# Attention's loads reshaped: rkT without empty partitions, u as one row, v split, two clearings moved

## The chip, the cores and the metric

One NeuronCore of a Trainium2 chip runs the whole program. Times are device microseconds (us) of one execution; lower is better. The kernel before took 453.38 us as the median of three runs (453.3 to 454.85).

## The reference

The program is a chain of three layers, all in float32.

1. Attention with a decaying state: 2 sequences, 8 heads, 768 tokens, head size 48. For each token t, `y_t = r_t (state + (u * k_t) v_t^T)`, then `state = w * state + k_t v_t^T`; u and w have one value for each head and channel.
2. A mixture of 8 experts with one choice per token (1536 tokens of 384 channels, 1024 hidden channels, relu, a capacity per expert), scaled by the softmax probability of the chosen expert.
3. A gated layer (silu of one product times another, then an output product; 1536 hidden channels).

Only the attention layer and the clearing of the experts' buffer are touched by the change.

## The kernel before

**Tiles.** The 1536 tokens are 12 tiles of 128. Two heads share the 128 partitions: head j of a pair sits on partitions 64j to 64j + 47, so partitions 48 to 63 and 112 to 127 are empty. A tile has three loads: `rkT` (r and k with channels on the partitions, 2 x 4 x 128 values in each, padded with zeros to 128 partitions on the host by `pad`, L1187), `rk` (r and k with tokens on the partitions) and `v`, which is loaded three tiles at a time (L139). `rkT` and `rk` have three buffers each.

**Start.** SyncE (SP) issues w_dm, then rkT, rk of tile 0, v of tiles 0 to 2, rkT and rk of tiles 1 and 2 (L126 to L156). ScalarE's (ACT's) queue issues u (one row of 384 values, read 128 times so that each partition has it), the routing weights `wg` and the capacity (L147 to L151). Meanwhile VectorE (DVE) and GpSimd (POOL) build `W2`, the powers of the decay and their inverses, by doubling (L206 to L225), and TensorE (PE) runs warm-up matmuls (L168), clears y and U in PSUM (L190) and sums a check over the partitions (`pbad`, L217), which DVE copies to `bad` (L227). PE then transposes the inverse powers to `wk_tok` (L233), which ACT copies (L234), and DVE copies u into a PSUM bank (`u_ps`, L339).

**The loop.** Python's loop over `it` from -4 to 12 (L380) writes the instructions of each engine in the order in which they run; each engine works through its own list in order and waits by semaphores. The steps of tile i are spread over iterations:

- `decay(i)` (L241, it = i - 3): DVE multiplies the whole rkT tile by W2 into `RK`, all 128 partitions; for tile 0 in two halves. After it SP may load rkT of tile i + 3 into the buffer (`load_T`).
- `diag_pool(i)` and `keys_pool(i)` (L247, L252, it = i - 4): POOL makes `ruk = r * k` and `kd = k * wk_tok`. After them SP may load rk of tile i + 3.
- `diag_dve(i)` (L256): DVE multiplies ruk by `u_ps` and sums per head to c. `diag_act(i)` (L264): ACT makes 8 diagonal blocks `AT` from c.
- `inner(i)` (L271): PE multiplies k and r of RK for each head (only the 48 used rows), and DVE writes the product's part under the mask into AT (`copy_predicated`, L283).
- `state_pe(i)` (L287): PE multiplies kd and v to U; `state_update(i)` (L296): DVE turns U into the next state Z, which for later tiles POOL finishes (L378).
- `outputs(i)` (L305): PE makes y from Z and RK and from v and AT; ACT copies y (L324); PE transposes it with the routing weights (L512); DVE routes a batch of tiles (L522 to L583).
- From iteration 4 on POOL scatters rows of finished tiles into the experts' buffer `x_disp` in memory (L597). Before that, the first 224 rows of expert 0 and of expert 1 are cleared by two DMAs of 336 KB from a zero tile, issued by SP in iterations -2 and 0 (L450 to L452). The clearings for later experts happen in the expert stage.
- From iteration 3 on SP also loads the first expert weights (`prefetch`).

After the loop come the experts (to about 212 us) and the gated layer.

Of the kernel before, what the change touches and what calls it, by code (L numbers as in the profile page):

```python
# [11 lines left out]
F32 = mybir.dt.float32  # L12
# [11 lines left out]
P = 128  # L24
B, H, S, D = 2, 8, 768, 48
NCH = S // P
NT = B * NCH
HP = H // 2
DM = H * D
# [5 lines left out]
ST = N + BLK  # L35
# [34 lines left out]
class Kernel:  # L70
# [47 lines left out]
    def attention(self, st):  # L118
        tc, nc, a = self.tc, self.nc, self.a
        tp = self.tp = self.pool(st, "tp")  # L120
        cp = self.cp
        ps_1 = self.ps_1 = self.pool(st, "ps_1", space=PSUM)
        NB = 3
# [3 lines left out]
        rkT = [tp.tile([P, 2, HP, P], F32, name=f"rkT{i}") for i in range(NB)]  # L127
        rk = [tp.tile([P, 2, DM], F32, name=f"rk{i}") for i in range(NB)]
        v_all = tp.tile([P, NT, DM], F32, name="v_all")

        def load_T(i):
            if i < NT:
                nc.sync.dma_start(out=rkT[i % NB], in_=a["rkT"][i])

        def load_rk(i):
            if i < NT:
                nc.sync.dma_start(out=rk[i % NB], in_=a["rk"][i])

        def load_v(i):  # L139
            nc.sync.dma_start(  # L140
                out=v_all[:, i:i + 3], in_=a["v"][i * P:(i + 3) * P].rearrange("(n p) d -> p n d", p=P)
            )

        load_T(0)
        load_rk(0)
        u_b = tp.tile([P, DM], F32, name="u_b")
        nc.scalar.dma_start(out=u_b, in_=a["u_row"].partition_broadcast(P))  # L147
        wg = tp.tile([P, HP * E], F32, name="wg")
        nc.scalar.dma_start(out=wg, in_=a["wg"].rearrange("p h e -> p (h e)"))
        cap_i = tp.tile([P, 2], I32, name="cap_i")  # L150
        nc.scalar.dma_start(out=cap_i, in_=a["cap"].bitcast(I32).partition_broadcast(P))  # L151
        load_v(0)
        load_T(1)
        load_rk(1)
        load_T(2)
        load_rk(2)  # L156

# [4 lines left out]
        ones = tp.tile([P, P], F32, name="ones")  # L162
        nc.vector.memset(ones, 1.0)

        def warm(n):
# [7 lines left out]
            out=tmpm, in_=ones, pattern=[[1, P]], compare_op=ALU.is_gt, fill=0.0, base=0, channel_multiplier=-1  # L173
# [9 lines left out]
        Z = [tp.tile([P, HP, D], F32, name=f"Z{i}") for i in range(2)]  # L183
        self.zero = cp.tile([P, DM], F32, name="zero")
        nc.vector.memset(self.zero, 0.0)
        y = ps_1.tile([P, HP, P], F32, name="y")
        U = ps_1.tile([P, HP, D], F32, name="U")

        for part in (y[:, 0:3], y[:, 3:], U):
            nc.tensor.matmul(  # L190
                part.rearrange("p h t -> p (h t)"), lhsT=ones, rhs=self.zero[:, 0:part.shape[1] * part.shape[2]],
                start=True, stop=True,
# [4 lines left out]
        u_ps = self.psum_rooms(True)  # L197
# [4 lines left out]
        W2 = tp.tile([P, 2, HP, P], F32, name="W2")  # L202
# [11 lines left out]
            out=neq, in0=sq[:, 0], scalar=1.0, in1=w_dm, op0=ALU.mult, op1=ALU.not_equal, accum_out=nbad  # L214
# [3 lines left out]
        for i in range(7):  # L218
            n = 1 << i
# [7 lines left out]
        nc.vector.tensor_copy(self.bad, pbad)  # L227


        wk_tok = tp.tile([P, DM], F32, name="wk_tok")  # L230
        wps = ps_1.tile([P, HP, 2, 64], F32, name="wps", tag="xt")
        for hp in range(HP):
# [3 lines left out]
        RK, AT, cc, ruks, decays = {}, {}, {}, {}, {}  # L236
# [4 lines left out]
        def decay(i):  # L241
            RK[i] = tp.tile([P, 2, HP, P], F32, name="RK", tag="RK", bufs=4)

            for h in (slice(0, 2), slice(2, HP)) if i == 0 else (slice(0, HP),):
                decays[i] = nc.vector.tensor_mul(RK[i][:, :, h], rkT[i % NB][:, :, h], W2[:, :, h])

        def diag_pool(i):  # L247
            r_t, k_t = rk[i % NB][:, 0], rk[i % NB][:, 1]
# [87 lines left out]
            for i in range(NT - NLAST, NT)  # L336
        }
        self.xr0 = self.hp.tile([BP, 2, DM], F32, name="xr", tag="xr", bufs=2)
        nc.vector.tensor_copy(u_ps, u_b)  # L339


        px = []
# [23 lines left out]
        def issue():  # L366

            i = self.scaled[0][0]
            self.issue()
            if i == NT - NLAST - 1:  # L370
                self.x_load(0, self.xr0)
# [8 lines left out]
        for it in range(-4, NT + 1):  # L380

            if self.to_scatter:
                self.scale()
                if it >= NT - 3:
                    issue()
            batch = ends.get(it - 1)
            late = it - 1 >= NT - LATE
            if ok(it - 1):
                self.logits(it - 1)
            if ok(it):  # L390
                outputs(it)
                if not late:
                    d_major(it)
            if it == 0:
                diag_act(2)
            if batch:
                self.route1(*batch)
            if late:
                if ok(it):
                    d_major(it)  # L400
                if it - 2 >= NT - LATE:
                    first_add(it - 2, it - 2 == NT - LATE, False)
                if it == NT:
                    for i in range(NT - NLAST, NT - LATE):
                        first_add(i, False, False)
                self.place_pe(*batch)
                self.route2(*batch)
                if it == NT:
                    first_rows(False)
                    first_add(NT - 1, False, True)  # L410
            if has_state(it + 1):
                state_update(it + 1)
            if ok(it + 3):
                decay(it + 3)
                load_T(it + 3 + NB)
            if it < 0 and ok(it + 2):
                inner(it + 2)
            if ok(it + 3):
                diag_dve(it + 3)

                if it != -1:
                    diag_act(it + 3)
            if it < 0 and ok(it + 4):
                diag_pool(it + 4)
            if has_state(it + 1) and (it + 1) % NCH:
                op = state_decay(it + 1)
                if ok(it + 3):
                    behind(op, decays[it + 3])
            if it >= 0 and ok(it + 4):
                behind(diag_pool(it + 4), decays[it + 3])  # L430
            if ok(it + 4):
                keys_pool(it + 4)
                load_rk(it + 4 + NB)
            if it >= 0 and ok(it + 2):
                inner(it + 2)
            if batch and not late:
                self.place_pe(*batch)
            if self.scaled:
                issue()

            if it == NT - 5 or it == NT - 3:
                self.scale()
                issue()
            if batch and not late:
                self.route2(*batch)
            if it == -1:
                self.route_inputs(wg, cap_i)
            if it in (-1, 2, 4):
                load_v({-1: 3, 2: 6, 4: 9}[it])
            if it in (-2, 0):  # L450
                first = (it + 2) // 2 * ST
                self.clear_rows(self.x_disp[first:first + BLK])  # L452
            if ok(it):
                self.token_major(it)
            if has_state(it + 2):
                state_pe(it + 2)
            self.prefetch(it)
            if it in WARMS:
                warm(WARMS[it])
# [722 lines left out]
def layout(inp):  # L1182
    r, k, v = (np.asarray(inp[n]) for n in "rkv")
    tok = lambda x: x.transpose(0, 2, 1, 3).reshape(N, DM)
    o = {}

    def pad(x):  # L1187

        z = np.zeros(x.shape[:2] + (64,) + x.shape[3:], x.dtype)
        z[:, :, :D] = x  # L1190
        return z.reshape((x.shape[0], P) + x.shape[3:])


    dm = lambda x: x.reshape(B, HP, 2, NCH, P, D).transpose(0, 3, 2, 5, 1, 4).reshape(NT, 2, D, HP, P)
    o["rkT"] = pad(np.stack([dm(r), dm(k)], axis=3))
    o["rk"] = np.ascontiguousarray(np.stack([tok(r).reshape(NT, P, DM), tok(k).reshape(NT, P, DM)], axis=2))
    o["v"] = np.ascontiguousarray(tok(v))
    w = np.asarray(inp["w"])
    o["w_dm"] = pad(w.reshape(1, HP, 2, D).transpose(0, 2, 3, 1))[0]
    o["w_row"] = np.ascontiguousarray(w.reshape(DM))  # L1200
    o["u_row"] = np.ascontiguousarray(np.asarray(inp["u"]).reshape(DM))
    o["wg"] = pad(np.asarray(inp["moe_w_gate"]).reshape(1, HP, 2, D, E).transpose(0, 2, 3, 1, 4))[0]
    o["cap"] = np.asarray(inp["moe_capacity"], dtype=np.int64).reshape(1)
    w1 = np.asarray(inp["moe_w1"])
    o["w1"] = np.ascontiguousarray(w1.reshape(E, KD, P, 4, 256).transpose(0, 3, 2, 1, 4)).reshape(E, 4, P, UC)
    w2 = np.asarray(inp["moe_w2"])
    o["w2"] = np.ascontiguousarray(w2.reshape(E, 4, 2, P, DM).transpose(0, 1, 3, 2, 4)).reshape(E, 4, P, UC)
    for n in ("w_gate", "w_val"):
        m = np.ascontiguousarray(np.asarray(inp["moe2_" + n], dtype=np.float64))
        o[n] = np.ascontiguousarray(  # L1210
            m.view(np.int64).reshape(KD, P, 6, 256).transpose(2, 1, 0, 3)
        ).reshape(6, P, KD * 256)
    m = np.ascontiguousarray(np.asarray(inp["moe2_w_out"], dtype=np.float64))
    o["w_out"] = np.ascontiguousarray(m.view(np.int64).reshape(6, 2, P, DM).transpose(0, 2, 1, 3)).reshape(6, P, 2 * DM)
    return o
# [17 lines left out]
```

## Time and profile before

| what | value |
|---|---|
| median of three runs | 453.38 us |
| profiled execution | 451.36 us, of which the span from first to last instruction 449.6 us |
| PE busy | 432.4 us (96% of the span) |
| DVE, ACT, POOL busy | 295.1, 212.4, 156.1 us |
| rkT loads | 12 of 512 KB, median 5.4 us from issue to landing |
| rk loads | 12 of 384 KB, median 6.4 us |
| clearings `x_disp<-zero` | 8 of 336 KB, median 7.1 us (two of them in the attention stage) |
| u load | 1 of 192 KB, 4.6 us |

How to read the rows further down: a line of a view in order of time has the start, the duration, the engine, the source line, the operation, what it writes and reads, and in square brackets how long the engine was idle before it and what ended that idle time. Engine names that end in q (SPq, ACTq) are the issuing of DMAs.

### The profile page before, as it was taken

To read this page: it belongs to the slowest core of one execution; us is meant where nothing else is said; L and a number is where in the kernel's file an instruction comes from. 1 tells how busy PE (TensorE), PEld (TensorE's weight loads), DVE (VectorE), ACT (ScalarE), POOL (GpSimd) and SP (SyncE) were. 2 spreads that over 40 slices of the span, in tenths; PEclk is the share of its full clock that TensorE was granted. 3 is DMA by queue.
4 is the path that set the end of the run, shared out by engine and by line. 5 is a ranking of instruction groups with operands and counts; after the bars stand their busy time and mean duration, and the time that the engine had idled before them with its cause. 6 is when DMAs were issued, how large, how long until landed. Compare 5 with 4: busy or idle time off the path is not lost. (4 is left out here: it accounts for less than half of the span.)

```text
span 449.6 us, 8438 instructions
## 1 busy us (share of the span) xinstructions
PE 432.4 (96%) x3211; PEld 418.3 (93%) x3211; DVE 295.1 (66%) x578; ACT 212.4 (47%) x469; POOL 156.1 (35%) x147
## 2 busy tenths in 40 slices
PE   7899999999999999999999999999999999999991
PEld 7788878989999999999998999999999999999991
DVE  7989986887877977986557888979865111111110
ACT  1687774636756756755555534343343031230310
POOL 5745652201121220000343555555546233332321
PEclk9899999999999999999999999999999999999996
DMA  7998942599999999602022423242300100001001
GB/s 255 315 357 281 398 165 85 161 362 261 330 219 266 203 293 275 231 1 72 1 70 71 137 85 125 77 140 81 131 2 0 53 1 19 36 0 54 2 20 40
DMA packets 24802, 63.78 MB, mean 142 GB/s; under 512 B 4784, under 2 KB 10032, under 8 KB 24752
## 3 DMA queue, kind: packets, MB, share of 16 engines
q1 hardware_dynamic: 22112, 57.43, 40.5%
q0 software_dynamic: 1920, 4.73, 2.9%
q10 hardware_dynamic: 720, 1.00, 0.8%
q8 instruction: 27, 0.44, 0.4%
q14 instruction: 23, 0.19, 0.1%
HBM read 55.67 MB, written 7.48 MB: 140 GB/s over the span
## 5 line engine op out<-in xcount | busy, mean ns | idle before, releaser
L1034 POOL TENSOR_TENSOR al<-sg,ah 128x384 fp32r<-128x384 f32 x48 | 54.1, 1128 | 132.9 <-ACT ah L1033 132.9
L667 DVE TENSOR_TENSOR wlo<-raw,whi 128x768 fp32r<-128x768 f32 x60 | 57.2, 954 | 9.4 <-ACT whi L666 8.5
L799 PE MATMUL py<-hc,whi 128*128 128x448 f32 x192 | 63.1, 370 | 0.0
L1033 ACT CAST ah<-sg 128x384 fp32r<-128x384 f32 x48 | 24.7, 514 | 78.0 <-DVE sg L1030 78.0
L810 PE MATMUL A<-xc,whi 128*128 128x224 f32 x336 | 57.7, 276 | 1.0 <-DVE xc L683 0.9
L800 PE MATMUL py<-hc,wlo 128*128 128x256 f32 x192 | 53.8, 280 | 0.0
L810 PEld LDWEIGHTS A<-xc,whi 128*128 128x128 f32 x336 | 51.2, 192 | 1.9 <-DVE xc L683 1.5
L666 ACT CAST whi<-raw 128x768 fp32r<-128x768 f32 x60 | 49.9, 838 | 0.7 <-PE py L799 0.7
L1047 PE MATMUL po<-w_out_hi,ah 128*128 128x384 f32 x144 | 48.6, 337 | 0.0
L1049 PE MATMUL po<-w_out_hi,al 128*128 128x384 f32 x144 | 48.5, 337 | 0.0
L1048 PE MATMUL po<-w_out_lo,ah 128*128 128x384 f32 x144 | 48.5, 337 | 0.0
L810 PE MATMUL A<-xc,wlo 128*128 128x224 f32 x168 | 46.2, 275 | 0.0
L877 POOL DMA_INDIRECT ids<-tok,by_expert x12 | 13.9, 1162 | 75.0 <-DMA ids<-tok,by_expert 66.6
L1056 DVE TENSOR_TENSOR acc<-acc,po 128x384 f32<-128x384 f32 x36 | 19.3, 546 | 30.9 <-PE po L1049 30.9
L799 PEld LDWEIGHTS py<-hc,whi 128*128 128x128 f32 x192 | 36.0, 188 | 2.6
L1030 DVE TENSOR_TENSOR sg<-A,sg 128x384 f32<-128x384 f32 x24 | 13.3, 555 | 37.0 <-PE A L1027 29.3
L800 PEld LDWEIGHTS py<-hc,wlo 128*128 128x128 f32 x192 | 36.5, 190 | 0.0
L1030 DVE TENSOR_TENSOR sg<-g,sg 128x384 f32<-128x384 f32 x24 | 13.3, 555 | 34.5 <-PE g L1027 27.6
L269 ACT ACTIVATE AT<-ident,c 128x128 f32<-128x128 f32 x96 | 29.3, 389 | 9.1 <-DVE c L260 9.0
L829 ACT ACTIVATE hc<-A 128x224 fp32r<-128x224 f32 x64 | 23.1, 362 | 21.3 <-PE A L810 18.6
L810 PEld LDWEIGHTS A<-xc,wlo 128*128 128x128 f32 x168 | 32.2, 192 | 0.0
L1029 ACT ACTIVATE sg<-A 128x384 f32<-128x384 f32 x24 | 11.6, 484 | 33.8 <-PE A L1027 33.8
(171 smaller groups left out, 1106.3 us busy)
## 6 DMA issues: line engine op xcount, KB each, us to landing
raw<-in_w SPq DMA_DIRECT2D x62, 384.0 KB, 6.8
rkT<-in_rkT SPq DMA_DIRECT2D x12, 512.0 KB, 5.4
rk<-in_rk SPq DMA_DIRECT2D x12, 384.0 KB, 6.4
raw<-in_w_gate SPq DMA_DIRECT2D x6, 768.0 KB, 4.2
raw<-in_w_val SPq DMA_DIRECT2D x6, 768.0 KB, 4.2
raw<-in_w_out SPq DMA_DIRECT2D x6, 768.0 KB, 4.3
x_disp<-zero SPq DMA_DIRECT2D x8, 336.0 KB, 7.1
xr<-x_disp SPq DMA_DIRECT2D x8, 336.0 KB, 6.1
```

What stands on the lines that cost most here:

```text
L269: nc.scalar.activation(AT[i][:, j, hp], ident, AF.Copy, scale=c[:, j, hp:hp + 1])
L666: nc.scalar.copy(h_, raw)
L667: nc.vector.tensor_sub(l_, raw, h_.bitcast(F32))
L799: nc.tensor.matmul(ps[:, 0:2 * BLK], lhsT=wh, rhs=xc, start=first, stop=False, skip_group_check=True)
L800: nc.tensor.matmul(ps[:, 0:256], lhsT=wl, rhs=xc[:, 0:256], start=False, stop=last, skip_group_check=True)
L810: self.nc.tensor.matmul(ph[:, HI], lhsT=w[:, k, fs], rhs=x[1][:, k, half], start=(k == 0 and i == 0), stop=(k == KD - 1 and i == 2),)
L1030: nc.vector.tensor_mul(sg, pg["w_val"], sg)
L1033: nc.scalar.copy(h_, sg)
L1034: nc.gpsimd.tensor_sub(l_, sg, h_.bitcast(F32))
L1047: nc.tensor.matmul(po, lhsT=ah[:, ts_], rhs=wh, start=(i == 0), stop=False)
L1048: nc.tensor.matmul(po, lhsT=ah[:, ts_], rhs=wl, start=False, stop=False)
L1049: nc.tensor.matmul(po, lhsT=al[:, ts_], rhs=wh, start=False, stop=(i == len(parts) - 1))
```

## The change

- `rkT` is stored without the padding, and each tile's load is two DMAs, one for the 48 rows of each half. The 16 empty rows between the halves are filled with zeros once for each of the three buffers, by DMAs on ACT's queue from the zero tile. `decay` works on partitions 0 to 111 instead of 128.
- u is loaded as one row on one partition, and one matmul with a row of ones copies it to all partitions of `u_ps`; the DVE copy is gone.
- v of tile 0 is loaded alone; v of tiles 1 and 2 is loaded after rk of tile 1.
- The two clearings of `x_disp` are issued in iterations 1 and 2 instead of -2 and 0.

```diff
--- before.py
+++ after.py
@@ -130,28 +130,30 @@
 
         def load_T(i):
             if i < NT:
-                nc.sync.dma_start(out=rkT[i % NB], in_=a["rkT"][i])
+                for j in range(2):
+                    nc.sync.dma_start(out=rkT[i % NB][64 * j:64 * j + D], in_=a["rkT"][i, j])
 
         def load_rk(i):
             if i < NT:
                 nc.sync.dma_start(out=rk[i % NB], in_=a["rk"][i])
 
-        def load_v(i):
+        def load_v(i, n=3):
             nc.sync.dma_start(
-                out=v_all[:, i:i + 3], in_=a["v"][i * P:(i + 3) * P].rearrange("(n p) d -> p n d", p=P)
+                out=v_all[:, i:i + n], in_=a["v"][i * P:(i + n) * P].rearrange("(n p) d -> p n d", p=P)
             )
 
         load_T(0)
         load_rk(0)
-        u_b = tp.tile([P, DM], F32, name="u_b")
-        nc.scalar.dma_start(out=u_b, in_=a["u_row"].partition_broadcast(P))
+        u_b = tp.tile([1, DM], F32, name="u_b")
+        nc.scalar.dma_start(out=u_b, in_=a["u_row"].rearrange("(o d) -> o d", o=1))
         wg = tp.tile([P, HP * E], F32, name="wg")
         nc.scalar.dma_start(out=wg, in_=a["wg"].rearrange("p h e -> p (h e)"))
         cap_i = tp.tile([P, 2], I32, name="cap_i")
         nc.scalar.dma_start(out=cap_i, in_=a["cap"].bitcast(I32).partition_broadcast(P))
-        load_v(0)
+        load_v(0, 1)
         load_T(1)
         load_rk(1)
+        load_v(1, 2)
         load_T(2)
         load_rk(2)
 
@@ -183,6 +185,11 @@
         Z = [tp.tile([P, HP, D], F32, name=f"Z{i}") for i in range(2)]
         self.zero = cp.tile([P, DM], F32, name="zero")
         nc.vector.memset(self.zero, 0.0)
+        for t in rkT:
+            nc.scalar.dma_start(
+                out=t[D:64].rearrange("p a (h i) t -> p (a h) (i t)", i=2),
+                in_=self.zero[0:64 - D, 0:256].unsqueeze(1).to_broadcast([64 - D, HP, 256]),
+            )
         y = ps_1.tile([P, HP, P], F32, name="y")
         U = ps_1.tile([P, HP, D], F32, name="U")
 
@@ -227,6 +234,7 @@
         nc.vector.tensor_copy(self.bad, pbad)
 
 
+        nc.tensor.matmul(u_ps, lhsT=ones[0:1], rhs=u_b, start=True, stop=True)
         wk_tok = tp.tile([P, DM], F32, name="wk_tok")
         wps = ps_1.tile([P, HP, 2, 64], F32, name="wps", tag="xt")
         for hp in range(HP):
@@ -241,8 +249,9 @@
         def decay(i):
             RK[i] = tp.tile([P, 2, HP, P], F32, name="RK", tag="RK", bufs=4)
 
+            rows = slice(0, 64 + D)
             for h in (slice(0, 2), slice(2, HP)) if i == 0 else (slice(0, HP),):
-                decays[i] = nc.vector.tensor_mul(RK[i][:, :, h], rkT[i % NB][:, :, h], W2[:, :, h])
+                decays[i] = nc.vector.tensor_mul(RK[i][rows, :, h], rkT[i % NB][rows, :, h], W2[rows, :, h])
 
         def diag_pool(i):
             r_t, k_t = rk[i % NB][:, 0], rk[i % NB][:, 1]
@@ -336,7 +345,6 @@
             for i in range(NT - NLAST, NT)
         }
         self.xr0 = self.hp.tile([BP, 2, DM], F32, name="xr", tag="xr", bufs=2)
-        nc.vector.tensor_copy(u_ps, u_b)
 
 
         px = []
@@ -447,8 +455,8 @@
                 self.route_inputs(wg, cap_i)
             if it in (-1, 2, 4):
                 load_v({-1: 3, 2: 6, 4: 9}[it])
-            if it in (-2, 0):
-                first = (it + 2) // 2 * ST
+            if it in (1, 2):
+                first = (it - 1) * ST
                 self.clear_rows(self.x_disp[first:first + BLK])
             if ok(it):
                 self.token_major(it)
@@ -1192,7 +1200,7 @@
 
 
     dm = lambda x: x.reshape(B, HP, 2, NCH, P, D).transpose(0, 3, 2, 5, 1, 4).reshape(NT, 2, D, HP, P)
-    o["rkT"] = pad(np.stack([dm(r), dm(k)], axis=3))
+    o["rkT"] = np.ascontiguousarray(np.stack([dm(r), dm(k)], axis=3))
     o["rk"] = np.ascontiguousarray(np.stack([tok(r).reshape(NT, P, DM), tok(k).reshape(NT, P, DM)], axis=2))
     o["v"] = np.ascontiguousarray(tok(v))
     w = np.asarray(inp["w"])
```

## Rows read from the trace of the kernel before

**Rows 1.** The page's first block: busy us (share of the span) and instructions.
```profile
PE 432.4 (96%) x3211; PEld 418.3 (93%) x3211; DVE 295.1 (66%) x578; ACT 212.4 (47%) x469; POOL 156.1 (35%) x147
```

**Rows 2.** Windows: stretch, its us, busy time of each engine, PEclk, DMA share, GB/s.
```profile
10.00:12.50 2.50, 2.36 (x34) 2.11 (x35) 2.28 (x4) 1.40 (x5) 1.17 (x2) 1.00 1.02 409
16.00:19.00 3.00, 3.00 (x37) 2.51 (x35) 2.57 (x4) 1.82 (x7) 3.00 (x3) 0.50 0.82 302
20.00:60.00 40.00, 39.07 (x592) 33.56 (x591) 37.23 (x89) 32.92 (x99) 22.52 (x26) 1.00 0.93 334
```

**Rows 3.** Order of time, DVE, the start of attention.
```profile
3.73 0.17 DVE L206 TENSOR_SCALAR sq<-w_dm 128x4 f32<-128x4 f32 x1 [0.93 <-DMA w_dm<-in_w_dm]
...
7.32 0.16 DVE L227 COPY bad<-pbad 128x1 f32<-128x1 f32 x1
7.40 0.55 DVE L339 COPY bank<-u_b 128x384 f32<-128x384 f32 x1
7.86 2.08 DVE L245 TENSOR_TENSOR RK<-rkT,W 128x512 f32<-128x512 f32 x2
...
11.11 1.23 DVE L245 TENSOR_TENSOR RK<-rkT,W 128x1024 f32<-128x1024 f32 x1
...
13.58 0.73 DVE L283 COPY_PREDICATED AT<-mask,A 128x512 f32<-128x512 uint8 x1 [0.44 <-ACT AT L269]
...
15.25 0.35 DVE L300 TENSOR_TENSOR Z<-U,sq 112x192 f32<-112x192 f32 x1
...
17.85 0.73 DVE L283 COPY_PREDICATED AT<-mask,A 128x512 f32<-128x512 uint8 x1 [0.43 <-ACT AT L269]
...
19.05 0.55 DVE L260 TENSOR_REDUCE c<-ruk 128x8 f32<-128x384 f32 x1
```

**Rows 4.** Order of time, PE.
```profile
7.01 0.28 PE L217 MATMUL pbad<-nbad,ones 128*128 128x1 f32 x2
...
15.74 0.84 PE L291 MATMUL U<-v_all,kd 128*48 128x48 f32 x16 [1.39 <-DVE Z L300]
```

**Rows 5.** Order of time, SP's DMA issues.
```profile
1.26 0.42 SPq L133 DMA_DIRECT2D rkT<-in_rkT  x1
...
2.20 0.43 SPq L140 DMA_DIRECT2D v_all<-in_v  x1
...
32.47 0.43 SPq L140 DMA_DIRECT2D v_all<-in_v  x1
```

**Rows 6.** Line 133 from 1 to 1.5 us: landing of tile 0's rkT after issue.
```profile
DMA to landing us min/median/max: 5.6/5.6/5.6
```

**Rows 7.** Order of time, POOL.
```profile
7.86 1.54 POOL L250 TENSOR_TENSOR ruk<-rk 128x384 f32<-128x384 f32 x1 [1.14 <-DMA rk<-in_rk]
9.36 1.45 POOL L254 TENSOR_TENSOR kd<-rk,wk_tok 128x384 f32<-128x384 f32 x1
12.13 1.06 POOL L250 TENSOR_TENSOR ruk<-rk 128x384 f32<-128x384 f32 x1 [1.33 <-DMA rk<-in_rk]
...
15.41 2.17 POOL L254 TENSOR_TENSOR kd<-rk,wk_tok 128x384 f32<-128x384 f32 x1
...
41.84 1.16 POOL L597 DMA_INDIRECT x_disp<-xu,row  x1 [0.17 <-issue]
```

**Rows 8.** Groups by shape, PE, 5 to 8 us: busy us, mean ns.
```profile
L190 PE MATMUL y<-zero,ones 128*128 128x384 f32 x2 | 0.8, 487 | 0.0
```

**Rows 9.** Order of time, ACT.
```profile
8.29 0.48 ACT L234 COPY wk_tok<-wps 128x384 f32<-128x384 f32 x1 [4.78 <-PE wps L233]
...
20.43 2.75 ACT L269 ACTIVATE AT<-ident,c 128x128 f32<-128x128 f32 x9
```

**Rows 10.** Line 670, 17.5 to 25 us: landing of the two clearings.
```profile
DMA to landing us min/median/max: 4.6/6.1/7.6
```

**Rows 11.** Line 140, 2 to 2.5 us: landing of the first v.
```profile
DMA to landing us min/median/max: 7.6/7.6/7.6
```

**Rows 12.** Waits of SP's queue, 0 to 8 us: us in total, times, longest.
```profile
SPq L137 <- DMA u_b<-in_u_row: 2.1, 1, 2.1
```

## The prediction

> **What bounds the kernel now.** I read the page's busy line first, then windows of the attention stage, then each engine's instructions in order of time from the start to 20 us. TensorE (PE) is busy for 96% of the span [rows 1], and from 20 to 60 us, where attention runs in its steady turn, for 39.07 of 40 us [rows 2]. The DMA engines are loaded there too (0.93), but no load is late: the reader will find no DMA named as a releaser in VectorE's (DVE's) rows after the first one. So a shorter load pays only before the steady turn.
>
> In that start I asked what DVE waits for. It begins when w_dm lands (3.73), builds the decay tables, copies `bad` at 7.32 after PE's `pbad` matmul (ends 7.29), copies u into PSUM at 7.40 for 0.55 us, and begins the first decay at 7.86 [rows 3, 4]. Tile 0 of rkT had landed at 1.26 + 5.6 = 6.86 [rows 5, 6]: this load was already covered. From 7.86 on DVE has two stops, 0.44 and 0.43 us, both on ScalarE's (ACT's) AT, none on a DMA [rows 3]. PE's unbroken work starts at 15.74, when DVE's Z of tile 0 (15.25 + 0.35 = 15.60) releases it [rows 3, 4]. So DVE's chain from 7.86 sets when the steady turn starts, and from there a shift should reach the end one to one, since PE stays the bound.
>
> GpSimd (POOL) does wait for loads: ruk of tile 0 starts when rk lands (7.86), ruk of tile 1 at 12.13 after 1.33 us of waiting [rows 7]. But that second one is done at 13.19 [rows 7], and DVE comes to it only after its mask copy at 13.58 + 0.73 = 14.31 [rows 3]. The wait has 1.1 us of cover.
>
> **The change part by part.**
>
> *u.* Removed: the DVE copy, 0.55 us, and 192 KB of load. Decay 0 can follow the `bad` copy as the u copy did, at 7.40: -0.46 us (7.86 - 7.40). It can't go earlier: `bad` waits for `pbad`, which PE reaches only after its warm-up. Added: one matmul of 384 columns, 0.8 us by the nearest row, the 384-column clearing of y [rows 8]. PE does it right behind `pbad`, so about 7.3 to 8.1; wk_tok's transposes come that much later and ACT's copy of them moves from 8.29 to about 8.75, done by 9.25 [rows 9]. POOL's kd of tile 0, which needs it, starts at 9.36 today because ruk goes before it [rows 7]: hidden, by about 0.1 us; past this cover it delays only kd 0, used by PE well before 15.74. DVE needs u in PSUM first after decay 0, after 9 us: hidden.
>
> *rkT without empty rows.* Each tile's 512 KB becomes twice 192 KB. At the 409 GB/s of 10 to 12.5 us [rows 2] that is 0.32 us less queue time a tile (128 KB), twelve times, none of it waited for now: 0 us. SyncE (SP) issues 12 more, about 0.4 us each [rows 5]; SP mostly waits for buffers, so 0. Each decay waits for two loads instead of one; rows don't show what a second wait costs DVE. Bounds: 0, and 0.2 us for each of the three decays before the steady turn, by the 0.16 us of DVE's smallest copies [rows 3]; I take 0, since the loads have landed.
>
> *Three fills of the empty rows*, issued on ACT's queue behind u, wg and cap. They are 64 KB each, and decay 0 now also waits for the first. The nearest load is w_dm: issued at 0.82, in use at 3.73, thus 2.9 us [rows 3]; issued at about 2.2, the fill lands at about 5.1, with 4.6 us (the shorter clearing of x_disp [rows 10]) at 6.8. Both are before 7.40: 0 us. What if it is issued late is rival 2.
>
> *v of tile 0 alone, the rest behind rk 1.* Tile 0's v lands sooner than 2.20 + 7.6 = 9.8 [rows 5, 11]. Tiles 1 and 2 are first read by PE at 15.74 [rows 4]; the load goes out right behind rk 1, which today is in by 12.13, and with fewer bytes ahead. 0 us.
>
> *Clearings three iterations later.* The two DMAs move behind the loads of iterations 1 and 2; the second goes out behind the v load that SP issues at 32.47 + 0.43 now [rows 5]. With 4.6 to 7.6 us to landing it is done at 37.5 to 40.5, before the first scatter on POOL at 41.84 [rows 7, 10]. Hidden, by 1.3 us at least; without that cover POOL would stand at the scatter. They leave the stretch from 18 to 25 us, where nobody waits for a DMA: 0 us.
>
> *What is late next.* DVE and POOL get in each other's way when both read two operands from SBUF: decay 0's two halves and ruk 0 start together at 7.86 and take 2.08 and 1.54 us, where later decays take 1.23 whole and ruk 1.06; kd of tile 2 takes 2.17 beside decay 2 [rows 3, 7]. With rk 1 earlier, ruk 1 can meet decay 1 (11.11, 1.23 us, alone today). If DVE is the one that stands, it loses up to 1.06, of which its stop of 0.44 takes part: +0.6; the same may happen once more at decay 2. Bounds 0 to +1.2; I take 0, by the row of kd of tile 2, in which POOL was the one held up.
>
> *PE's clock.* From 16 to 19 us it was granted at 0.50, the lower level of 1.2 GHz, after PE had stood before 15.74 for 1.39 us; from 20 us it is full [rows 2, 4]. If the shift keeps it up, ACT's second AT batch could start when its c is ready (19.05 + 0.55 = 19.60) rather than at 20.43 behind y: up to -0.8 [rows 3, 9]. If one more such stretch appears, PE loses half of 3.00 us: +1.5. The stop itself stays, so I take 0.
>
> Sum: -0.46 us. The profiled execution took 451.36 us (449.6 of span and 1.76 around it), so 450.9 on its scale; the runs' median, 453.38, is 2.02 above it, and on that scale the forecast is 452.9. Its own range is 452.1 (-0.46 - 0.8) to 455.0 (-0.46 + 0.6 of extra waits, 1.2 of collisions, and a fifth of the clock's 1.5).
>
> **Rivals.**
>
> 1. *Loads lead the start.* For: DMA share of 1.02 from 10 to 12.5 us [rows 2], and POOL's waits for rk. Before rk 1 lands, 2 x 128 + 192 + 384 = 832 KB go away, 2.1 us at 409 GB/s. If all behind moves by that, and the clock stays up (0.8): 453.38 - 2.9 = 450.5. Against: DVE never stops for a load after 7.86 [rows 3].
>
> 2. *The fill of tile 0 is issued late (slower).* SP's load of rk 1 stood 2.1 us until u's load had landed [rows 12], with just eight DMAs ahead of it: a new load waits for an old one. The change issues 18 before the loop in place of 11, and the fills are the last on ACT. If the first stands behind v 0, which lands at 9.8 less 704 KB (u, a quarter of rkT 0, two thirds of v) at 409 GB/s, so 8.0, and needs 2.9 more, decay 0 starts at 10.9, not 7.86: 456.5. Behind it on ACT stand two fills, the table load and the wk_tok copy. It decides from a landing later than 7.40. Against: ACT issues few DMAs, so its fourth should find an early, small one ahead of it.
>
> 3. *The queue becomes the bound of the steady turn.* If a load into 48 rows ran at half the 409 GB/s, an rkT pair would take 1.92 us where 512 KB takes 1.28; six tiles from 20 to 60 us add 3.8 us, the clearing that moves in 0.84 (336 KB), to 0.93 x 40 = 37.2 us: 41.9, 1.9 over: 454.8. Against: loads are issued three tiles ahead and none is waited for. The Trainium skill, "SBUF — State Buffer", section "Door 1: The DMA port swizzle", speaks for it: by it 64 partitions of one half reach 8 of 16 ports and get hardly more than 32 do, and two transfers to the halves don't add up. No row of the kernel before shows a load of that shape.
>
> **How the numbers follow.** Forecast 0.70, rival 1 0.14, rival 2 0.10, rival 3 0.06. A measurement of this kernel can tell about 0.5%, 2.27 us, from no change: bounds 451.1 and 455.65. Rival 1 is faster (0.14), rival 2 with a little of the forecast's tail slower (0.11), the rest the same (0.75). The range goes from rival 1's 450.5 to the forecast's upper end, 455.0, which takes in rival 3 and leaves out rival 2 and tails, some 0.15.
>
> **What will show it.** Right: decay 0 within 0.1 us of 7.4, no DVE stop on a DMA, PE's Z release near 15.1, the steady turn as long as now, the scatter without a wait. Wrong: decay 0 released by a DMA (rival 2), Z released more than 1.5 us sooner (rival 1), DVE or PE waiting for rkT, rk or v between 20 and 60 us (rival 3), decay 1 or 2 much over 1.23 us (the collisions, here costed at nothing).

## The result and the profile after

The changed kernel takes 459.5 us (median of 6 runs, 457.83 to 460.79). The kernel before, run on the same chip between them, takes 453.19 us. The ratio is 1.0126, with a 95% interval of 1.0098 to 1.0154: slower, by 1.3%. The forecast of 452.9 and its range of 450.5 to 455.0 are both missed. The profiled execution after took 458.27 us with a span of 456.5 us, 6.9 more than the span before.

**Is PE still the bound?** First the page's busy line and the windows, as in [rows 1, 2].

```profile
PE 435.5 (95%) x3213; PEld 420.5 (92%) x3213; DVE 294.0 (64%) x577; ACT 212.6 (47%) x469; POOL 155.1 (34%) x147
```

```profile
5.00:7.50 2.50, 2.50 (x15) 2.22 (x15) 0.57 (x4) 0.61 (x1) 0.58 (x2) 1.00 1.06 238
10.00:12.50 2.50, 2.27 (x33) 2.02 (x34) 1.62 (x4) 1.31 (x5) 0.89 (x1) 1.00 1.02 287
...
20.00:22.50 2.50, 2.50 (x40) 2.26 (x40) 2.47 (x4) 2.47 (x8) 1.34 (x3) 1.00 1.04 247
22.50:25.00 2.50, 2.50 (x46) 2.09 (x41) 2.24 (x6) 2.39 (x9) 1.93 (x3) 1.00 1.04 237
...
27.50:30.00 2.50, 0.04 (x1) 0.00 (x0) 0.93 (x3) 2.50 (x9) 0.17 (x1) 0.96 1.07 255
30.00:32.50 2.50, 0.94 (x18) 0.88 (x20) 0.00 (x0) 0.01 (x1) 0.00 (x0) 0.50 1.05 246
32.50:35.00 2.50, 2.50 (x24) 2.10 (x26) 2.42 (x4) 0.00 (x0) 0.54 (x2) 0.50 1.01 273
20.00:60.00 40.00, 35.27 (x503) 30.18 (x505) 31.69 (x74) 27.94 (x85) 19.13 (x22) 0.91 0.96 263
```

Read the last two columns together: the busy share of the DMA engines, and the bytes that they moved. The DMA engines are full (share 1.0) in every short stretch shown, and yet move only 237 to 287 GB/s. In the kernel before, a full queue moved 409 [rows 2], and two of the stretches above were these (windows of the kernel before):

```profile
20.00:22.50 2.50, 2.50 (x42) 2.22 (x42) 2.47 (x5) 2.50 (x9) 1.28 (x2) 1.00 0.86 263
...
30.00:32.50 2.50, 2.50 (x42) 2.22 (x41) 1.94 (x4) 2.46 (x8) 2.06 (x3) 1.00 1.03 417
```

There the queue had room at 20 us (0.86). After the change it carries fewer bytes, has no room, and falls behind. From 20 to 60 us PE is busy for 35.27 us where it was 39.07.

**Where PE stands.** Order of time, PE, after:

```profile
26.41 1.14 PE L520 MATMUL xl<-IW,xT 128*128 128x104 f32 x8 [0.69 <-ACT xT L333]
31.56 0.88 PE L300 MATMUL U<-v_all,kd 128*48 128x48 f32 x16 [4.02 <-DMA v_all<-in_v]
32.37 1.95 PE L320 MATMUL y<-RK,Z 48*48 48x128 f32 x16
34.25 1.95 PE L326 MATMUL y<-AT,v_all 128*48 128x128 f32 x16
36.12 1.39 PE L285 MATMUL A<-RK 48*128 48x128 f32 x16
37.44 1.14 PE L520 MATMUL xl<-IW,xT 128*128 128x104 f32 x8
```

PE waits 4.02 us for v of tiles 3 to 5. The y groups behind the wait take 1.95 us each, where the undisturbed ones take 1.08 (below, with the fifth experiment), because PE's granted clock is at its lower level, 0.50 or 1.2 GHz, in the windows after the stop. In the kernel before, the same U group began at 27.30 with no wait:

```profile
27.30 0.56 PE L291 MATMUL U<-v_all,kd 128*48 128x48 f32 x16
...
30.91 1.14 PE L512 MATMUL xl<-IW,xT 128*128 128x104 f32 x8
```

The second line is the next xl group. So U is 31.56 - 27.30 = 4.26 us later and xl 37.44 - 30.91 = 6.53 later; the 2.27 between them is the lower clock. These 6.53 us make up nearly all of the span's 6.9.

**Why v is late.** SP's issues of that load, after:

```profile
20.86 0.35 SPq L138 DMA_DIRECT2D rk<-in_rk  x1
21.25 1.37 SPq L141 DMA_DIRECT2D v_all<-in_v  x1
```

Before, its issue and its landing (line 140, 20 to 21 us) were these:

```profile
20.48 0.46 SPq L140 DMA_DIRECT2D v_all<-in_v  x1
```

```profile
DMA to landing us min/median/max: 6.7/6.7/6.7
```

thus 27.18, only 0.12 us before PE used it. After, it goes out 0.8 us later and takes 10.3 us, if the end of PE's wait (31.56) is taken as its landing, which this trace doesn't give. The load had almost no slack to give.

**The start.** DVE after, against [rows 3]:

```profile
7.47 0.16 DVE L234 COPY bad<-pbad 128x1 f32<-128x1 f32 x1 [1.35 <-PE pbad L224]
7.94 2.10 DVE L254 TENSOR_TENSOR RK<-rkT,W 112x512 f32<-112x512 f32 x2 [0.31 <-DMA rkT<-zero]
...
11.94 1.23 DVE L254 TENSOR_TENSOR RK<-rkT,W 112x1024 f32<-112x1024 f32 x1 [0.85 <-DMA rkT<-in_rkT]
...
15.36 0.35 DVE L309 TENSOR_TENSOR Z<-U,sq 112x192 f32<-112x192 f32 x1
```

The u copy is gone, but decay 0 waits 0.31 us for the fill of the empty rows, and decay 1 waits 0.85 us for rkT. Z of tile 0 comes at 15.36 (15.25 before). POOL's ruk of the first three tiles wait for rk and start at 8.28, 12.69 and 16.88, where the kernel before has 7.86, 12.13 [rows 7] and 14.46:

```profile
8.28 1.21 POOL L259 TENSOR_TENSOR ruk<-rk 128x384 f32<-128x384 f32 x1 [2.62 <-DMA rk<-in_rk]
...
12.69 1.33 POOL L259 TENSOR_TENSOR ruk<-rk 128x384 f32<-128x384 f32 x1 [1.79 <-DMA rk<-in_rk]
...
16.88 1.08 POOL L259 TENSOR_TENSOR ruk<-rk 128x384 f32<-128x384 f32 x1 [1.89 <-DMA rk<-in_rk]
```

PE's U of tile 1 starts at 15.80, where it was 15.74 [rows 4]:

```profile
15.80 0.64 PE L300 MATMUL U<-v_all,kd 128*48 128x48 f32 x16 [0.78 <-POOL kd L263]
```

The row names POOL's kd, but that kd had ended by 14.98 (13.98 + 1.00). What ended just ahead of U is Z of tile 0, at 15.71 (15.36 + 0.35); Z released it in the kernel before too [rows 4]. The start gains nothing and loses next to nothing; the loss is at 27 us.

### The profile page after: what moved, and what is told of

It reads as the page before. It is cut to its first block, busy times and chain, and to the rows that moved or that the text cites. A ratio compares the mean times of both kernels' runs of the same rounds, so it can differ in the third digit from the quotient of the medians.

```text
span 456.5 us, 8466 instructions
## 1 busy us (share of the span) xinstructions
PE 435.5 (95%) x3213; PEld 420.5 (92%) x3213; DVE 294.0 (64%) x577; ACT 212.6 (47%) x469; POOL 155.1 (34%) x147
```

## The experiments

Two explanations stood at the outset. **A:** a DMA into 48 rows moves its bytes at about half the rate, so each rkT pair holds the queue longer than the padded tile did. **B:** it is the number of DMAs (SP issues 12 more, each with its own fixed cost, and a new one waits for an old one), not their shape.

**1. rkT padded again, the rest of the change kept.**

```diff
-                for j in range(2):
-                    nc.sync.dma_start(out=rkT[i % NB][64 * j:64 * j + D], in_=a["rkT"][i, j])
+                nc.sync.dma_start(out=rkT[i % NB], in_=a["rkT"][i])
...   (no fills, decay on 128 rows)
```

> The changed kernel with only rkT's part undone: padded rows again, one load of 128 rows a tile, no fills; u, v and the clearings stay changed. Half-rate theory (loads into 48 rows move bytes at about half the rate, so the queue runs full from 5 to 32 us and v of tiles 3 to 5 lands late): the wait of 4.0 us before the product of kd and v of tile 3 is gone, 452 to 453.2 us. Issue theory (the number of DMAs in flight is what delays them): also close to before, 453 to 454. Theory that v's split, u or the clearings' place make the loss: stays at 458 to 460.

Measured: 453.1 us against 453.54, ratio 0.9984 (0.9956 to 1.0012). The loss is gone. DVE, then PE:

```profile
7.41 2.09 DVE L248 TENSOR_TENSOR RK<-rkT,W 128x512 f32<-128x512 f32 x2
...
14.81 0.35 DVE L303 TENSOR_TENSOR Z<-U,sq 112x192 f32<-112x192 f32 x1
```

```profile
15.76 1.89 PE L314 MATMUL y<-RK,zero 48*48 48x128 f32 x16
17.58 1.88 PE L320 MATMUL y<-AT,v_all 128*48 128x128 f32 x16
...
26.77 0.56 PE L294 MATMUL U<-v_all,kd 128*48 128x48 f32 x16
```

Decay 0 starts at 7.41 and Z at 14.81, 0.45 and 0.44 us sooner than in [rows 3]: the u step of the prediction, in full. The U group that waited 4.02 us has no wait here, and starts 0.53 us sooner than in the kernel before. The gain is too small for the interval, and in this trace it doesn't last: the last U group starts at 60.39, as in the kernel before. In versions 3 and 7 it starts at 59.71 and 59.41, so there a lead is left.

**2. The rkT edit alone, with its fills, on the kernel before.**

```diff
-                nc.sync.dma_start(out=rkT[i % NB], in_=a["rkT"][i])
+                for j in range(2):
+                    nc.sync.dma_start(out=rkT[i % NB][64 * j:64 * j + D], in_=a["rkT"][i, j])
+        for t in rkT:
+            nc.scalar.dma_start(out=t[D:64]..., in_=self.zero...)
...   (decay on 112 rows, no padding on the host)
```

> The kernel before with only rkT's part: 48-row pairs and the fills. Half-rate and issue theory: v of tiles 3 to 5 late by 4 us or more, because the clearing at iteration -2 is still ahead of it too; 458 to 461 us. Theory that v's split, u or the clearings make the loss: 452.5 to 453.5.

Measured: 458.24 us, ratio 1.0123 (1.0093 to 1.0152): the whole loss from this part of the change. PE:

```profile
31.30 0.56 PE L297 MATMUL U<-v_all,kd 128*48 128x48 f32 x16 [1.81 <-DMA v_all<-in_v]
```

The same load is late. The route differs a little: here more of the delay comes in the start (DVE's decay 1 stands 1.50 us for rkT and begins at 13.80, 11.11 before), so less is left to wait for at 31 us.

**3. Two DMAs a tile again, but each of 128 rows.** One carries r, the other k, 256 KB each; 24 DMAs as in the changed kernel.

```diff
-                    nc.sync.dma_start(out=rkT[i % NB][64 * j:64 * j + D], in_=a["rkT"][i, j])
+                    nc.sync.dma_start(out=rkT[i % NB][:, j], in_=a["rkT"][i, :, j])
...   (padded on the host, no fills, decay on 128 rows)
```

> The changed kernel, rkT padded again, but still two DMAs a tile, split into the r columns and the k columns, each of 128 rows and 256 KB: as many DMAs as the changed kernel and a third more bytes, but each over all partitions. Half-rate theory: no late v, 452.3 to 453.5 us. Issue theory (twice as many DMAs with a bound on how many are in flight): late as in the changed kernel, 458 to 460.

Measured: 452.96 us, ratio 0.9991 (0.9965 to 1.0016). As many DMAs, more bytes, no loss. Theory B falls.

**4. The loads by themselves.** A kernel that only loads: six tiles of 4 KB a row in each of several shapes, one shape after another.

```diff
+    def rows(i, lo, n, q):
+        q.dma_start(out=t[i][lo:lo + n], in_=a[i, lo:lo + n])
+    whole: rows(i, 0, 128, sync)           low48:  rows(i, 0, 48, sync)
+    pair:  rows(i, 0, 48, sync); rows(i, 64, 48, sync)
+    pair_two_queues: the same, the second on ACT's queue
+    rows112: rows(i, 0, 112, sync)         rows96: rows(i, 0, 96, sync)
```

> Loads alone, nothing of the reference is computed: seven stretches of six tiles each from memory, one after the other (128 rows of 4 KB in one DMA, twice; pairs of 48 rows from one queue; pairs from two queues; 112 rows in one DMA; 48 low rows; 96 rows in one DMA). Half-rate theory: whole tiles at about 400 GB/s, pairs from one queue at about 200, 48 low rows at about 200, 112 and 96 rows between. Pairs from two queues tell whether the halves can be moved side by side: 200 if not, up to 400 if so. Issue theory: all shapes at about the same rate once in flight.

Windows inside each stretch (its us; DVE and POOL busy; PEclk; DMA share; GB/s), in this order: 128 rows, pairs of 48, pairs on two queues, 112 rows, the low 48 rows alone, 96 rows.

```profile
16.50:22.50 6.00, 0.00 (x0) 0.00 (x0) 1.00 1.02 411
27.00:36.50 9.50, 0.00 (x0) 0.00 (x0) 1.00 1.04 193
42.00:50.50 8.50, 0.00 (x0) 0.00 (x0) 1.00 1.03 215
55.00:62.50 7.50, 0.00 (x0) 0.00 (x0) 1.00 1.03 279
67.50:73.00 5.50, 0.00 (x0) 0.00 (x0) 1.00 0.97 150
78.00:84.50 6.50, 0.00 (x0) 0.00 (x0) 1.00 0.99 268
```

All six are full by their share, at rates from 150 to 411 GB/s. A padded tile takes 512 KB / 411 GB/s = 1.28 us; a pair takes 384 KB / 193 GB/s = 2.04 us. Theory A holds, and the difference, 0.76 us a tile, is an addition where the prediction had a saving of 0.32. Six rkT tiles are issued ahead of the late v load: 6 x 0.76 = 4.6 us, the size of its lateness (4.3). The sum isn't exact, since u and one clearing leave the queue ahead of it and the fills come in.

The rates also give those of the changed kernel: one pair and one rk load (384 KB at 411 GB/s, 0.96 us) are 768 KB in 3.0 us, about 262 GB/s, where its windows have 237 to 287. What the three fills add is not separated, since experiments 1 and 3 leave them out with the pairs and no run has them alone. But the rate is as low without them: the third tile's decay, which needs the last of them, has started by 15.88, and from 20 to 25 us the full queue moves 247 and 237.

**5. PE kept busy inside the wait.** Idle matmuls on a constant, as those at the kernel's start, ahead of the U group that waits.

```diff
+            if it == 1:
+                warm(14)
```

> The changed kernel with 14 warm-up matmuls (128 columns, about 3.7 us by the 1.60 us that six take) put in front of the product of kd and v of tile 3, where PE stands 4.0 us for v; they compute nothing that is used. Theory that the loss is the wait and then the clock (after the wait PE ran at the lower level until about 37 us: y took 1.95 twice instead of 1.08, U 0.88 instead of 0.56): v lands as late, at about 31.6, but the clock stays full and some 2.3 us come back: 456 to 457.5 where the changed kernel has 459.5. Theory that the whole loss is the late load: no gain, 459 to 460.

Measured: 457.0 us, ratio 1.0084 (1.0051 to 1.0118). PE:

```profile
27.85 3.31 PE L170 MATMUL A<-ones 128*128 128x128 f32 x28
31.58 0.56 PE L300 MATMUL U<-v_all,kd 128*48 128x48 f32 x16 [0.42 <-DMA v_all<-in_v]
32.08 1.08 PE L320 MATMUL y<-RK,Z 48*48 48x128 f32 x16
...
35.19 1.14 PE L522 MATMUL xl<-IW,xT 128*128 128x104 f32 x8
```

v lands as late as before (U at 31.58), but the clock stays up, the y group takes 1.08 and xl starts at 35.19 in place of 37.44: 2.25 us back in the trace, 1.0126 - 1.0084 = 0.0042, about 1.9 us, in the ratio. The intervals of the two ratios overlap, so it is the trace that shows the gain. So the loss has two parts: some 4.3 us of late data and some 2 us of clock behind it.

**6. v of tiles 3 to 5 issued one iteration sooner.**

```diff
-            if it in (-1, 2, 4):
-                load_v({-1: 3, 2: 6, 4: 9}[it])
+            if it in (-2, 2, 4):
+                load_v({-2: 3, 2: 6, 4: 9}[it])
```

> The changed kernel with one thing moved: v of tiles 3 to 5 is issued one iteration earlier, ahead of rkT 5 and rk 6 (768 KB, some 3.3 us at the 230 to 250 GB/s of that stretch). Theory that one late load sets the loss: v lands at about 28, the wait shrinks from 4.0 us to under 1, the clock stays up, 453 to 454.5 us. Theory that the queue as a whole is the bound from 5 to 32 us: another load (rkT 5 or rk 5) is late in its place, by 2 us or more, and the time stays at 456 or above.

Measured: 454.4 us, ratio 1.0031 (1.0004 to 1.0058). Three quarters of the loss go with one line moved. PE:

```profile
28.32 0.59 PE L300 MATMUL U<-v_all,kd 128*48 128x48 f32 x16 [0.21 <-DMA v_all<-in_v]
28.84 1.95 PE L320 MATMUL y<-RK,Z 48*48 48x128 f32 x16
30.71 1.76 PE L326 MATMUL y<-AT,v_all 128*48 128x128 f32 x16
```

The wait is down to 0.21 us. What remains is mostly the clock: 1.95 + 1.76 - 2 x 1.08 = 1.55 us, beside the 1.4 us (0.0031 x 453) of the ratio. PE had stood 1.58 us in front of its xl group at 26.97, for ACT's xT, so even this version has stops. The time is that of the first theory, but the clock did not stay up as it wanted. Of the second theory's wait for another load 0.56 us is there (DVE for an rkT), not 2 or more.

**7. Version 1 with four idle matmuls in PE's stop of the startup.** The kernel before has this stop too, in front of 15.74 [rows 4], and the prediction valued its clock at up to 0.8 us.

```diff
+            if it == -1:
+                warm(4)
```

> The changed kernel with rkT padded again (as in the run before with 453.1), and four warm-up matmuls (about 1.1 us) where PE stands 1.3 us at 14 us before the product of tile 1. If PE's stop is what drops the clock for the next 3 us, the clock stays up, y of tile 0 takes 1.08 and not 1.89 us twice, and ACT's second batch of AT starts up to 0.8 us sooner: 451.8 to 452.8 us. If the clock falls all the same, 452.8 to 453.5.

Measured: 451.68 us against 452.63, ratio 0.9975 (0.9949 to 1.0001). PE:

```profile
15.82 1.08 PE L314 MATMUL y<-RK,zero 48*48 48x128 f32 x16
16.82 1.08 PE L320 MATMUL y<-AT,v_all 128*48 128x128 f32 x16
17.84 1.16 PE L279 MATMUL A<-RK 48*128 48x128 f32 x16
```

The two y groups take 1.08 where version 1 has 1.89 and 1.88, and ACT's AT batch of tile 2 (the prediction's second) starts at 19.10, where version 1 has 20.02 and the kernel before 20.43 [rows 9]. The u step and this one together, 0.46 + 0.8 = 1.26 us of 453, would be a ratio of 0.9972. The interval takes in 1 and that of version 1, so the gain of the idle matmuls is shown by the trace alone.

**8. The same with four more at the end of the recurrence.**

```diff
+                if it == NT - 2:
+                    warm(4)
```

> The version of e7_pad_warm (rkT padded to 128 rows again, four idle matmuls in PE's stop of the second startup iteration) with four more idle matmuls at the end of the recurrence, ahead of the matmul that places the recurrence's result, where PE stops for about 1 us at 67 us. Theory A: that stop drops the granted clock in some executions (in the trace of e1_pad_back the stretch from 70 to 73 us ran at the lower level, about 1.9 us more; in that of the kernel before it did not). Then the spread of the times narrows and the median comes to 450.3 to 451.3 us, a ratio of 0.994 to 0.997. Theory B: the fall at 70 us has another cause, or lies beside other work: the same as e7_pad_warm, 451 to 452 us, a ratio of 0.996 to 0.999, and the trace again shows 1.9 us for a y matmul group near 71 us in some executions.

Measured: 451.68 us against 452.93, ratio 0.9971 (0.9946 to 0.9997); the times run from 450.22 to 452.81, those of version 7 from 450.32 to 455.33 (one run; the next is 452.77). The median is where version 7 has it, not at the 450.3 to 451.3 that theory A of this run wanted. The window from 70 to 75 us of version 1, then of this one:

```profile
70.00:75.00 5.00, 5.00 (x43) 4.07 (x40) 1.47 (x10) 1.31 (x4) 1.92 (x2) 0.66 0.21 79
```

```profile
70.00:75.00 5.00, 4.77 (x40) 4.33 (x41) 2.87 (x19) 1.93 (x5) 2.12 (x3) 1.00 0.26 93
```

The clock of 0.66 isn't there in the second, but version 7's profiled execution had 1.00 there too without the added matmuls. Whether they prevent it stays open. Against the kernel before, this is the one version whose interval lies below 1, by some 0.3%.

## Why the prediction was wrong

- **The step that failed** is "rkT without empty rows": "At the 409 GB/s of 10 to 12.5 us [rows 2] that is 0.32 us less queue time a tile (128 KB), twelve times, none of it waited for now: 0 us." Both halves of it were wrong. The rate of a 128-row load was carried over to a 48-row one; measured, it is 193 GB/s, and the tile costs 0.76 us more (experiment 4). Experiments 1 to 3 put the loss on this part of the change and not on the number of DMAs. And the time was waited for, because v of tiles 3 to 5 had 0.12 us to spare. In place of 0 us the step cost nearly the whole loss: U came 4.26 us late, with 2.27 us of clock behind it.
- **The cover wasn't priced.** That no DMA was named as a releaser of DVE or PE in the kernel before said that no load was late for them; it did not say by how much each was early. "Loads are issued three tiles ahead and none is waited for" was the argument against rival 3. It is not true of this v load: it is issued in iteration -1 and used in iteration 1. The landing of each load against its first use would have shown it; the prediction did this for the clearings and for v of tiles 0 to 2, not for this one.
- **Rival 3** named the mechanism (half rate in 48 rows) and the sign (PE waiting for v between 20 and 60 us), and got 0.06. Its 454.8 was too low for two reasons: it started counting at 20 us, while the queue is full from 5 us on and six tiles' excess has piled up by the v load, and it had no term for the clock after PE's stop (2.27 us). The Trainium skill had the shape right, on the page "SBUF — State Buffer": by its section "Door 1: The DMA port swizzle" 64 partitions of one half move hardly more than 32, and by its section "Can I just issue two DMAs to hit both halves?" two halves don't add up. The pair's 193 GB/s agrees; two queues in place of one gave 215, 11% more. The Trainium skill, "DMA: Bandwidth & Descriptors", section "Rules for kernel authors", says of two transfers to the two halves not to bother and to use one of 128 partitions. Experiment 1 agrees by the ratio, 0.9984 in place of 1.0126.
- **u: -0.46 us** was right in size (-0.45 in experiment 1), but in the changed kernel the fill of tile 0 took 0.31 us of it back. That is rival 2 in small: the fill landed at about 7.9, not at 5.1 to 6.8, far from that rival's 10.9; "0 us" for the fills was wrong by this. The rest went because PE's `pbad`, and so the `bad` copy, came 0.15 us later (7.47 for 7.32). The 0.85 us that decay 1 stood for rkT cost little more, since DVE's stop of 0.44 us on ACT's AT [rows 3] went away. That a shift of the start reaches the end one to one isn't shown: the lead of experiment 1 is gone at 60 us.
- **Rival 1**, a start led by loads, went the other way: the loads got slower, and decay 1 began to wait.
- **Clearings, v 0 and collisions at 0** stand: the first scatter on POOL started 0.17 us after the instruction before it, as in [rows 7]; the first three decays took 2.10, 1.23 and 1.23 us, as in [rows 3]; experiment 1, which keeps all three edits, is not slower.
- **The clock: "I take 0", up to +1.5.** The stop in the startup stayed, as said. That a late load makes a second one was inside the term but tied to nothing, and it cost 2.27 us, more than the 1.5.

## What to carry to other kernels

Leaving out padding is a saving only if the DMA keeps its shape: here 33% more bytes in one DMA of 128 rows took 1.28 us, and the bare bytes in two DMAs of 48 rows 2.04. A "DMA share" near 1 doesn't tell how much room there is; read it beside GB/s, and list each load's landing beside its first use before calling it covered. A stop of PE can cost more than its length: behind the one here, the next 5 us ran at the lower clock and added 2.3 us to a wait of 4.0.

## What was not expected of the hardware

A single DMA of 112 rows ran at 279 GB/s and one of 96 rows at 268, against 411 for 128 rows with the same 4 KB a row: 448 KB take longer (1.64 us) than 512 KB (1.28 us). No run here shows why. The low 48 rows alone ran at 150 GB/s, less than the pair's 193.
